# One strip task, longer assumed DMA latencies, planned clearing of V and an own buffer for fill blocks in a list-scheduled two-layer transformer kernel

## Chip, cores and metric

The kernel runs on one core of one Trainium2 chip. The metric is the device time of the whole program in microseconds (us). Several runs are quoted as a median with lowest and highest; ratios between kernels are explained in the result.

## The reference, cut to what matters

```python
def _A_ref(x, mem0, Wq, Wk, Wv, Wo, seg_len):     # attention with a recurrent memory
    mem = mem0                                    # 8 rows
    for s in range(n_seg):                        # 64 segments of 32 rows
        h = jnp.concatenate([mem, xs], axis=1)    # 40 rows, 512 columns
        q, k, v = ...                             # 32 heads of 128
        p = softmax(masked scores)
        o = (p @ v) @ Wo
        mem = o[:, :M, :]                         # the next segment needs it
        outs.append(o[:, M:, :])
def _B_ref(x, w_gate, w_up, w_down):
    return (sigmoid(x @ w_gate) * (x @ w_up)) @ w_down     # 512 -> 1792 -> 512
x = x + _A_ref(_layernorm(x), ...); x = x + _B_ref(_layernorm(x), ...)   # layer 1
x = x + _A_ref(_layernorm(x), ...); x = x + _B_ref(_layernorm(x), ...)   # layer 2, same weights
```

Inputs are bfloat16, x is 2048 by 512. The memory makes the 64 segments of a layer a chain. Layer 2 may run at the same time as layer 1, some segments behind it.

## The kernel before

A step handles one segment of layer 1 and, six steps behind, one of layer 2. There are 70 steps; in the first and last six only one layer has work, and matmuls have 40 instead of 80 columns. The kernel first records all work as tasks (engine, assumed duration, assumed latency until others see the result, what is read and written). A planner then simulates the engines and fixes the order of every engine. On the chip the order is fixed; real waits are semaphores. So an assumed latency costs nothing by itself: it decides only what stands before what.

```python
class Planner:
    LAT = {"PE": 205.0, "DVE": 110.0, "ACT": 128.0, "POOL": 40.0, "SP": 2200.0}
# ... setup
        self.xp = [self.xo[0], c.tile([P, D], BF16, name="xp1")]    # fill blocks; xo is the output tile too
        for t_ in self.qku:
            nc.gpsimd.memset(t_[:], 0.0)
        for t_ in self.vsb:
            nc.gpsimd.memset(t_[:], 0.0)
# ... in each step: V of the memory rows, with 32-column weights, four matmuls side by side
        def strips(q):
            for c in range(DC):
                for i in range(4):
                    k = 2 * i + q
                    nc.tensor.matmul(vb[q][32 * i:32 * i + 32, :], lhsT=hT[:, c, SCOL:SCOL + 32], rhs=self.wv[:, c, k * 512:(k + 1) * 512],
                                     start=(c == 0), stop=(c == DC - 1), skip_group_check=True)

        def add_strips():
            sb = pl.buf(self.sstp)
            for q in range(2):
                pl.add("PE", DC * (mm_ns(512) + 12) + 75, lambda q=q: strips(q), r=..., w=[vb[q]], use=[sb])
            for q in range(2):
                pl.add(("ACT", "DVE"), copy_ns(512), lambda q=q: (sb[:, q, :], vb[q][:, :]), ...)
            for i in range(4):                       # spread the strips into the V tiles
                pl.add("SP", 430, lambda i=i, vu=vu: nc.sync.dma_start(
                    out=self.vsb[vu][32:64, :], in_=sb[32 * i:32 * i + 32, :, :]), ..., lat=2600.0, use=[sb])
```

The other rows of V do not depend on the memory. They are computed ahead (V passes), stored to a scratch tensor in HBM (scr) and loaded into vsb before the step that needs them. For layer 2 that is a recurrence: feed-forward of a block in layer 1, V pass, store, load, product with the probabilities six steps later. A V pass of layer 2 fills 96 of 128 rows; the free 32 take a third of a "fill block" of layer 1 (blocks 6, 9, 12, 15), which so needs x loaded and normalized on its own.

Line numbers below: L674 strips, L704 q and k, L718 scores, L777 transposed probabilities, L788 their product with V, L805 output projection, L904 and L928 feed-forward, L568 V passes, L538 transposes. In the changed kernel all these are two or three lower: L672, L701, L715, L774, L785, L802, L901, L925, L566, L536. Tiles in the lines of the profile: sst holds the strips on their way to vsb, pb the probabilities, ptsb the transposed ones, otsb their product with V, xn a normalized input, hT a step's transposed input, xvf and xvl inputs of V passes, vst a finished part of V on its way to scr.

## Time and profile before

| | before |
|---|---|
| time, 3 runs | 1903.02 us (1902.42 to 1903.92) |
| profiled span | 1905.1 us, mean granted TensorE clock 0.992 |
| PE busy, idle | 1853.5 us, 51.6 us |
| VectorE, ScalarE, GpSimd busy | 67%, 63%, 30% |
| matmuls | 41250 |

"PE busy" is the union of the matmuls' slices, and ends are modelled: a lone matmul's slice is 0.2 us long, though its follower can start after 0.04 us. So a stall shorter than that leaves no idle time, and a longer one shows that much less. Starts are the better measure.

### The profile page before, as it was taken

To read this page: it belongs to the slowest core of one execution; us is meant where nothing else is said; L and a number is where in the kernel's file an instruction comes from. 1 tells how busy PE (TensorE), PEld (TensorE's weight loads), DVE (VectorE), ACT (ScalarE), POOL (GpSimd) and SP (SyncE) were. 2 spreads that over 40 slices of the span, in tenths; PEclk is the share of its full clock that TensorE was granted. 3 is DMA by queue.
4 is the path that set the end of the run, shared out by engine and by line. 5 is a ranking of instruction groups with operands and counts; after the bars stand their busy time and mean duration, and the time that the engine had idled before them with its cause. 6 is when DMAs were issued, how large, how long until landed. Compare 5 with 4: busy or idle time off the path is not lost.

```text
span 1905.1 us, 94394 instructions
## 1 busy us (share of the span) xinstructions
PE 1853.5 (97%) x41250; PEld 1579.6 (83%) x41250; DVE 1284.5 (67%) x4214; ACT 1192.4 (63%) x2722; POOL 580.1 (30%) x824
## 2 busy tenths in 40 slices
PE   7999899999999999989999999999999999999998
PEld 3578788988988888979888888988888898988786
DVE  5456577776777667756766777767776677766664
ACT  5655567666666666656665666666666666666554
POOL 5412012332424142332413232232413232333311
PEclk9999999999999999999999999999999999999999
DMA  9733324554635454544635454464635444454534
GB/s 350 243 92 106 86 61 141 149 155 118 185 106 165 116 168 127 155 138 128 179 84 172 120 155 140 128 178 134 174 97 167 128 137 141 134 161 138 161 94 139
DMA packets 133965, 273.84 MB, mean 144 GB/s; under 512 B 29254, under 2 KB 65358, under 8 KB 133550
## 3 DMA queue, kind: packets, MB, share of 16 engines
q0 software_dynamic: 59104, 181.61, 32.7%
q1 hardware_dynamic: 74446, 86.19, 15.7%
q8 instruction: 323, 5.29, 1.2%
q14 instruction: 92, 0.75, 0.1%
HBM read 222.04 MB, written 27.26 MB: 131 GB/s over the span
## 4 chain that ended last, share of the span: by engine, by line
PE 87%; DMA 4%; DVE 4%; issue 2%; ACT 2%; SPq 1%; POOL 1%; ACTq 0%; POOLq 0%; DVEq 0%
PE bank L704 30%; PE bank L805 15%; PE bank L904 10%; PE bank L568 8%; PE bank L674 6%; PE bank L928 5%; PE bank L718 5%; PE bank L788 4%; PE bank L777 3%; DMA vsb<-sst 2%; PE bank L538 1%; DMA scr<-vst 1%; DMA xo<-in_A_x_dram 1%; SPq L685 1%; DVE st L731 0%
## 5 line engine op out<-in xcount | busy, mean ns | idle before, releaser
L704 PE MATMUL bank<-hT,wq_sb 128*128 128x80 bf16 (+1 forms) x8960 | 624.8, 198 | 2.8 <-DVE hT L823 0.8
L704 PE MATMUL bank<-hT,wk_sb 128*128 128x80 bf16 (+1 forms) x8960 | 623.4, 198 | 0.4 <-issue 0.4
L996 ACT CAST qku<-bank 128x480 bf16<-128x480 f32 (+3 forms) x770 | 394.6, 512 | 259.3 <-PE bank L704 233.4
L704 PEld LDWEIGHTS <-wq_sb 128*128 128x128 bf16 x8960 | 458.5, 99 | 30.0 <-issue 10.0
L704 PEld LDWEIGHTS <-wk_sb 128*128 128x128 bf16 x8960 | 451.2, 99 | 1.3 <-issue 1.3
L731 DVE TENSOR_TENSOR st<-bank,maskb 80x240 f32<-80x240 f32 (+1 forms) x732 | 269.5, 369 | 196.0 <-PE bank L718 187.3
L805 PE MATMUL bank<-otsb,wo_sb 128*128 128x80 bf16 (+1 forms) x8960 | 375.7, 199 | 3.5 <-ACT otsb L996 2.7
L805 PEld LDWEIGHTS <-wo_sb 128*128 128x128 bf16 x8960 | 341.9, 100 | 14.2 <-issue 4.6
L896 POOL DMA_DIRECT2D wg<-in_B_w_gate_dram x217 | 164.4, 757 | 479.4 <-PE bank L904 430.1
L996 ACT CAST otsb<-bank 128x480 bf16<-128x480 f32 (+3 forms) x420 | 198.7, 486 | 106.2 <-PE bank L788 75.1
L922 POOL DMA_DIRECT2D wd<-in_B_w_down_dram x217 | 154.0, 711 | 221.1 <-PE bank L928 171.2
L526 POOL TENSOR_TENSOR lns<-lns,negh 128x1 f32<-128x1 f32 (+1 forms) x79 | 49.0, 621 | 531.0 <-DVE lns L525 430.1
L760 DVE TENSOR_TENSOR pb<-st,rz 80x480 bf16<-80x480 f32 x348 | 206.0, 593 | 4.4
L743 DVE TENSOR_REDUCE sm<-st 80x6 f32<-80x240 f32 (+3 forms) x420 | 152.8, 364 | 71.7 <-ACT st L741 69.6
L741 ACT ACTIVATE st<-st 80x240 f32<-80x240 f32 (+3 forms) x420 | 159.9, 381 | 27.5 <-DVE st L738 24.5
L718 PE MATMUL bank<-qku 128*80 128x80 bf16 (+1 forms) x2240 | 173.6, 203 | 1.3 <-ACT qku L996 0.3
L718 PEld LDWEIGHTS <-qku 128*80 128x80 bf16 (+1 forms) x2240 | 128.3, 117 | 55.4 <-ACT qku L996 17.0
L904 PE MATMUL bank<-xnT,wu 128*128 128x128 bf16 (+2 forms) x1784 | 171.3, 218 | 1.3 <-DMA wu<-in_B_w_up_dram 1.3
L904 PE MATMUL bank<-xnT,wg 128*128 128x128 bf16 (+2 forms) x1784 | 172.1, 219 | 0.0
L996 ACT CAST ptsb<-bank 128x480 bf16<-128x480 f32 (+3 forms) x277 | 134.5, 495 | 50.9 <-PE bank L777 46.8
L788 PE MATMUL bank<-ptsb,vsb 128*128 128x80 bf16 (+1 forms) x2240 | 141.7, 199 | 24.2 <-DMA vsb<-sst 10.4
L897 POOL DMA_DIRECT2D wu<-in_B_w_up_dram x217 | 163.0, 751 | 5.3 <-PE bank L904 1.6
(103 smaller groups left out, 2578.0 us busy)
## 6 DMA issues: line engine op xcount, KB each, us to landing
wg<-in_B_w_gate_dram POOLq DMA_DIRECT2D x219, 256.0 KB, 4.3
wd<-in_B_w_down_dram POOLq DMA_DIRECT2D x219, 256.0 KB, 4.8
wu<-in_B_w_up_dram POOLq DMA_DIRECT2D x218, 256.0 KB, 4.9
vsb<-scr SPq DMA_DIRECT2D x512, 48.0 KB
vsb<-sst SPq DMA_DIRECT2D x280, 64.0 KB
scr<-vst SPq DMA_DIRECT2D x128, 96.0 KB
wv_sb<-in_A_Wv_dram SPq DMA_DIRECT2D x4, 1024.0 KB
wq_sb<-in_A_Wq_dram SPq DMA_DIRECT2D x5, 768.0 KB
```

Source lines behind the costliest of these rows:

```text
L704: nc.tensor.matmul(o_ap, lhsT=W[:, c, h * P:(h + 1) * P], rhs=mv(c), start=(c == 0), stop=(c == DC - 1))
L718: nc.tensor.matmul(s_all(SB)[pr, uh - h0 + i, :], lhsT=qku[:, i, 0, 0:ncol], rhs=qku[:, i, 1, 0:ncol], start=True, stop=True)
L731: pl.add("DVE", dve_ns(n, True), lambda gsz=gsz, hs=hs, st=st, SB=SB, pj_=pj_, npj_=npj_, mk=mk, idx=idx: nc.vector.tensor_tensor(out=st[p ...
L741: pl.add("ACT", act_ns(n), lambda hs=hs, st=st: nc.scalar.activation(out=st[pr, hs], in_=st[pr, hs], func=ACTF.Exp, scale=self.scale), r=s ...
L760: nc.vector.tensor_tensor(out=o, in0=st[pr, hs].unsqueeze(1).to_broadcast([npart, 2, gsz, L]), in1=rz[pr, :, 0:gsz].unsqueeze(3).to_broadc ...
L788: nc.tensor.matmul(OB[:, hl * ncol:(hl + 1) * ncol], lhsT=self.vsb[(4 * t + h // 8) % 5][:, (h % 8) * P:(h % 8 + 1) * P], rhs=ptsb[:, hl, ...
L805: nc.tensor.matmul(WB[:, c * ncol:(c + 1) * ncol], lhsT=self.wo[:, h, c * P:(c + 1) * P], rhs=otsb[:, hl, 0:ncol], start=(h == 0 and c == ...
L896: pl.add("POOL", 760, lambda wg=wg, fs=fs: nc.gpsimd.dma_start(out=wg[:], in_=self.wgv[:, :, fs]), r=[("wo", self.H - 1)], w=[gk] + bt, la ...
L897: pl.add("POOL", 760, lambda wu=wu, fs=fs: nc.gpsimd.dma_start(out=wu[:], in_=self.wuv[:, :, fs]), r=[("wo", self.H - 1)], w=[uk] + bt, la ...
L904: nc.tensor.matmul(gu[:, 2 * i + k, 0:n], lhsT=W[:, c, i * P:(i + 1) * P], rhs=xnT[:, c, rw], start=(c == 0), stop=(c == DC - 1))
L922: pl.add("POOL", 760, lambda wd=wd, ip=ip: nc.gpsimd.dma_start(out=wd[:], in_=self.wdv[:, 2 * ip:2 * ip + 2, :]), w=[dk] + (["boot"] if se ...
L996: nc.scalar.copy(out=dst, in_=src)
```

## The change

The intent: keep the strips together, tell the planner how long DMAs really take, take clearing out of the fixed preamble, and free the fill blocks from the output tile. Cut to its core (the weights' latency is changed in four places, one shown):

```diff
-    LAT = {"PE": 205.0, "DVE": 110.0, "ACT": 128.0, "POOL": 40.0, "SP": 2200.0}
+    LAT = {"PE": 205.0, "DVE": 110.0, "ACT": 128.0, "POOL": 40.0, "SP": 4000.0}
 ...
-        self.xp = [self.xo[0], c.tile([P, D], BF16, name="xp1")]
+        self.xp = c.tile([P, D], BF16, name="xp")
 ...
         for t_ in self.hT:
-            nc.vector.memset(t_[:], 0.0)
-        for t_ in self.qku:
-            nc.gpsimd.memset(t_[:], 0.0)
+            nc.vector.memset(t_[:, :, L:2 * L], 0.0)
         for t_ in self.pb:
             nc.vector.memset(t_[:], 0.0)
-        for t_ in self.vsb:
-            nc.gpsimd.memset(t_[:], 0.0)
+        for k, t_ in enumerate(self.vsb):
+            self.pl.add("POOL", 950, lambda t_=t_: nc.gpsimd.memset(t_[:], 0.0), w=[("vs", k), ("vx", 0, k), ("vx", 1, k)])
 ...                                                                  # V stores
-                       lambda vs=vs, d=d, c0=c0, n=n: ("dma", d, vs[c0:c0 + BLK * n, 0:512 * w]), lat=2600.0 + 1500.0 * boot,
+                       lambda vs=vs, d=d, c0=c0, n=n: ("dma", d, vs[c0:c0 + BLK * n, 0:512 * w]), lat=4000.0 + 500.0 * boot,
 ...
-            i = self.nxt("xp", 2)
-            xb, key = self.xp[i], (("xo", 0) if i == 0 else "xp1")
+            xb, key = self.xp, "xp"
 ...
-        def strips(q):
-            for c in range(DC):
-                ...
+        def strips():
+            for q in range(2):
+                for c in range(DC):
+                    ...
-            for q in range(2):
-                pl.add("PE", DC * (mm_ns(512) + 12) + 75, lambda q=q: strips(q), r=hkeys + [("wv", h) for h in range(H)], w=[vb[q]], use=[sb])
+            pl.add("PE", 2 * DC * (mm_ns(512) + 12) + 150, strips, r=hkeys + [("wv", h) for h in range(H)], w=vb, use=[sb])
 ...                                                                  # strips into vsb
-                       r=[(sb, 0), (sb, 1)], w=[("vs", vu)], lat=2600.0, use=[sb])
+                       r=[(sb, 0), (sb, 1)], w=[("vs", vu)], lat=3500.0, use=[sb])
 ...                                                                  # weights, four places
-                pl.add("POOL", 760, lambda wg=wg, fs=fs: nc.gpsimd.dma_start(out=wg[:], in_=self.wgv[:, :, fs]), r=[("wo", self.H - 1)], w=[gk] + bt, lat=4000.0)
+                pl.add("POOL", 760, lambda wg=wg, fs=fs: nc.gpsimd.dma_start(out=wg[:], in_=self.wgv[:, :, fs]), r=[("wo", self.H - 1)], w=[gk] + bt, lat=6000.0)
```

## The prediction

> **What bounds the kernel now.** I read the page first, for the engines and the clock.
>
> ```profile
> PE 1853.5 (97%) x41250; PEld 1579.6 (83%) x41250; DVE 1284.5 (67%) x4214; ACT 1192.4 (63%) x2722; POOL 580.1 (30%) x824
> ...
> PE   7999899999999999989999999999999999999998
> ```
>
> TensorE (PE) is the bound: 97% busy in a 1905.1 us span, no other engine over 67%, idle 1905.1 - 1853.5 = 51.6 us. The table by stretch shows where: 23.8 us before 300 us, 19.4 us in the 1500 us after that, 9.3 us after 1800 us. So nothing that frees VectorE, ScalarE or GpSimd counts by itself. Only two things can: idle time of PE, and time that PE spends inside its "busy" on nothing. The waits of PE name the first kind, longest first:
>
> ```profile
> PE bank L788 <- DMA vsb<-sst: 10.4, 14, 2.1
> PE bank L509 <- DVE ident L445: 7.8, 1, 7.8
> PE bank L788 <- DVE ptsb L998: 7.7, 5, 5.7
> PE bank L538 <- ACT xn L529: 5.1, 3, 3.4
> ...
> PE bank L788 <- DMA scr<-vst: 1.8, 1, 1.8
> PE bank L904 <- DMA wu<-in_B_w_up_dram: 1.3, 1, 1.3
> ```
>
> Columns: total us, times, longest us. L788 is the product of probabilities and V. It waits 14 times for the strips of V that a DMA spreads from sst into vsb. For the second kind I read PE's instructions in order of time, start to start:
>
> ```profile
> 421.87 0.31 PE L704 MATMUL bank<-hT,wk_sb 128*128 128x80 bf16 x4
> 422.11 1.05 PE L674 MATMUL bank<-wv_sb,hT 128*32 128x512 bf16 x16
> 423.08 0.54 PE L718 MATMUL bank<-qku 128*80 128x80 bf16 x9
> ```
>
> Groups of four L704 follow each other every 0.14 to 0.15 us, but the strips (L674) start 0.24 us after the last: 0.10 us lost going in, none of it shown as idle. The 16 strip matmuls then take 0.97 us. The chain that ended last gives the same 0.98 us for 16 alone, and 1.84 us for 32 in one piece: 2 x 0.98 - 1.84 = 0.12 us is what leaving costs.
>
> **What the Trainium skill says.** "TensorEngine Tiling (Array Packing)", Key Properties: changing the tiling mode drains TensorE. Strips are the only matmuls with 32-column weights (128*32 above), so each group changes mode twice; the 0.10 and 0.12 us agree. "Perfetto Trace Analysis", Identifying the Most-Contended Engine: matmul busy share is no measure of what is left; true here, the drains lie inside the 97%. "DMA: Bandwidth & Descriptors", Anatomy of one DMA, fits about 2.0 us fixed plus bytes over 436 GB/s, for GpSimd-issued transfers. That is 2.15 us for 64 KB, but the strip transfers, issued from SyncE, end waits after 3.23, 4.90 and 5.04 us in the chain (at 429.61, 452.26, 584.26 us). The trace decides: the old plan's 2.6 us was short, 3.5 us is nearer and still short of some. "SBUF — State Buffer", Who interferes with whom: a VectorE cast in a 2-port mode and a GpSimd instruction exclude each other. The start of the trace shows it:
>
> ```profile
> 3.10 4.51 POOL L467 MEMSET vsb<- 128x1024 bf16 x5
> ...
> 3.66 4.04 DVE L445 CAST ident<-st 128x128 bf16<-128x128 f32 x1
> ```
>
> The cast of the identity lasts 4.04 us and ends 0.1 us after the last vsb clearing; PE's first matmul waits for it (7.8 us above).
>
> **The change part by part.** A list scheduler fixes every engine's order at build time from assumed durations, so most of the change is a new order. I compared the two built orders. PE has 41250 matmuls in both, the same by line.
>
> 1. *One strip task.* Before, the 70 steps' strips stand in 113 groups (27 of 32 matmuls, 86 of 16); after, in 70 groups of 32. 43 groups fewer x (0.10 to 0.13 in + 0.12 out, say 0.24) = **10.3 us**, all on PE, spread evenly. PE's runs of one line rise from 3032 to 3066, but other changes cost about 0.02 us each in the timeline: 0.7 us back or more.
>
> 2. *Longer latencies, strips to L788.* I added the PE work that stands between a step's last strip and its first L788, at the trace's rates (48 L704 in 1.72 us, 8 of 512 columns in 1.73 us, 16 L904 in 0.89 us). Before: median 4.4 us, 55 of 70 steps under 5.0 us, least 2.9. After: median 5.8 us, 2 of 70 under 5.0 us, least 4.1. Needed: a copy (0.59 us) plus 3.2 to 5 us landing plus queueing. So most of the 10.4 us goes: estimate **8 us**.
>
> 3. *Stores of V at 4.0 instead of 2.6 us, weights at 6.0 instead of 4.0 us.* These waits are worth 1.8 and 1.3 us. The last V store still has 7.5 us of PE work or so before its reader, as before. Gain **2.5 us**. The weights land in 4.3 to 4.9 us by the page, so 6.0 is cautious: it costs time in the plan, not on the chip unless the order gets worse.
>
> 4. *A buffer for fill blocks.* Fill blocks 6 and 12 used xo, which is also the output buffer.
>
> ```profile
> 806.02 4.09 DMA out_dram<-xo
> 810.11 0.02 issue
> 810.13 5.58 DMA xo<-in_A_x_dram
> ...
> 815.73 0.69 DVE lns L523
> 816.43 0.23 DVE ptsb L998
> ```
>
> The load waits for the store, VectorE stands behind the load, and the ptsb copy that PE needs stands behind VectorE: 5.7 us of PE idle, once. With its own buffer the load for that block is issued far ahead. The first fill block (90 us) costs PE 1.1 us in the same way; in the new order its statistics stand after the three ptsb copies. **6.8 us**.
>
> 5. *Clearing.* Three GpSimd qku memsets (0.49 us each alone, about 0.44 in a row) leave the queue, vsb's five stay ahead of everything: the identity cast can end 1.3 us earlier, and the start with it. **1.3 us**. The smaller hT memsets are VectorE time while it waits anyway: 0.
>
> Sum: 10.3 + 8 + 2.5 + 6.8 + 1.3 = 28.9 us. A new order of 41250 matmuls also brings waits that no view can show ahead; the old one had about 20 us in 1500 us of steady running, partly counted above. I put **5 us** against the sum: 1903 - 28.9 + 5 = **1879 us**, 1.3% faster.
>
> **The rivals.** *The recurrence becomes the bound.* Block b of layer 1 must pass the feed-forward, V, its store and its load before step 4b + 6 of layer 2. Cautious latencies could push that work late and PE would idle. For it: the feed-forward's tiles are triple-buffered and their planned pace falls. Against: the PE work between a block's last V pass and its reader is 5.0 to 7.5 us after, 6.8 to 8.4 before, nearly the same, and PE was over 98% busy from 300 to 1800 us. If it happened: waits of L788 on vsb<-scr, 10 to 30 us, no gain or a small loss. *The strip's wait was hidden anyway, or moves to ScalarE.* One task takes two banks at once and asks for two copies together, so L788 could wait on the copies. For: SyncE already waits 501.4 us for ACT's sst copies. Against: the distances in 2 are measured from the last strip. Then about 1888 us. *More comes back than counted*: fewer waits let feed-forward work fill the layer-1-only steps before 260 us, where much of the idle lies. Boot V work does move later in the new order (272 of 288 matmuls before the end of the first step, 260 after). Then 1865 us or less. *The clock*: it was 0.91 and 0.83 around 120 to 160 us; a denser PE could be throttled more, 2 to 5 us back.
>
> **Range and chances.** Items 1 and 4 (17 us) rest on counts and one clear chain, the other 12 us are likelier to be partly given back. With 4 to 20 us of new waits, or a few us more of gain, I get 1864 to 1894 us for 8 in 10. Faster by 2% needs under 1865 us, 38 us, nearly three quarters of all PE idle, so 0.12; slower by 2% would need the recurrence to break, 0.01.
>
> **What would show it.** Right: L674 in 70 pieces of 1.84 us and no isolated 0.98 us; the wait of L788 on vsb<-sst at 3 us or less; no VectorE wait for out_dram before a fill block; identity cast ending near 6.4 us; PE busy near 1843 us, idle near 37 us. Wrong: PE waiting on vsb<-scr or wg, wu, wd; a clock under 0.985; idle of PE not below 50 us; or a gain over 38 us, which would mean drains or hidden gaps bigger than 0.24 us a group.

## The result, and the profile after

| | before | after |
|---|---|---|
| time | 1903.01 us (1902.42 to 1903.92, 4 runs) | 1881.94 us (1877.41 to 1887.37, 4 runs) |
| profiled span | 1905.1 us | 1881.1 us |
| mean granted clock, profiled run | 0.992 | 0.996 |
| PE busy, idle | 1853.5, 51.6 us | 1838.7, 42.4 us |

The ratio is 0.989 (95% interval 0.9863 to 0.9917): the mean time of one kernel's fast runs over that of the other's of the same rounds, so not quite the ratio of the medians above. It is about 21 us, within the predicted range and within 2%.

The page of the changed kernel, engines, and PE by slice:

```profile
PE 1838.7 (98%) x41250; PEld 1582.1 (84%) x41250; DVE 1284.4 (68%) x4221; ACT 1176.9 (63%) x2715; POOL 576.9 (31%) x820
...
PE   7999999999999999999999999999999999999999
```

The 8s are gone and PE is still the bound. The waits of PE (columns: total us, times, longest us):

```profile
PE bank L785 <- DMA vsb<-scr: 6.8, 3, 2.8
PE bank L507 <- DVE ident L445: 6.4, 1, 6.4
PE bank L536 <- ACT xn L527: 5.8, 5, 3.4
PE bank L802 <- ACT otsb L993: 5.3, 11, 1.4
PE bank L774 <- DVE pb L757: 2.5, 10, 0.5
PE bank L701 <- DVE hT L815: 2.2, 6, 0.4
PE bank L785 <- DMA vsb<-sst: 1.8, 4, 0.7
```

Read against the list of before: the strips' wait (vsb<-sst) fell from 10.4 to 1.8 us, the wait for VectorE's ptsb copy from 7.7 to 0.2 us (below the lines shown), the identity from 7.8 to 6.4 us. New at the top is vsb<-scr, the recurrence, which had no wait in the list of before, and the output projection's wait for ScalarE doubled from 2.7 to 5.3 us. The strips, in order of time:

```profile
442.54 0.31 PE L701 MATMUL bank<-hT,wk_sb 128*128 128x80 bf16 x4
442.78 1.91 PE L672 MATMUL bank<-wv_sb,hT 128*32 128x512 bf16 x32
444.62 0.42 PE L715 MATMUL bank<-qku 128*80 128x80 bf16 x6
```

The way in costs 0.10 us as before (0.24 us after the start of the last four L701, where such groups follow each other in 0.14), then 32 matmuls take 1.84 us. The start, GpSimd and VectorE:

```profile
3.57 2.73 POOL L465 MEMSET vsb<- 128x1024 bf16 x3
...
3.00 3.38 DVE L445 CAST ident<-st 128x128 bf16<-128x128 f32 x1
```

The cast still ends with the clearing, now at 6.38 us. PE's first V pass starts at 12.62 us, before at 13.95 us.

### The clock

What the prediction did not put in its sum is the clock. These are stretches of the trace of before around the stall of 5.7 us at 810 us (columns: stretch, length, busy time with counts of PE, PEld, DVE, ACT, POOL, then granted clock, DMA share, GB/s):

```profile
814.00:816.00 2.00, 0.00 (x0) 0.00 (x0) 0.27 (x1) 0.00 (x0) 0.00 (x0) 1.00 0.96 302
816.00:818.00 2.00, 1.29 (x21) 1.29 (x21) 1.22 (x5) 0.29 (x1) 0.00 (x0) 0.58 0.24 77
818.00:820.00 2.00, 2.00 (x24) 1.47 (x23) 0.23 (x1) 0.43 (x2) 0.00 (x0) 0.57 0.06 18
820.00:822.00 2.00, 2.00 (x58) 2.00 (x56) 0.45 (x2) 0.74 (x2) 1.28 (x2) 1.00 0.26 51
```

After the stall the granted clock is little more than half over some 4 us. The stall costs its idle time and then 2 x 0.42 + 2 x 0.43 = 1.7 us of clock, as much as 3.4 us at half clock. In steps of 10 us the trace of before has nine places under full clock (130 to 160, 190, 810, 970, 1810, 1870 and 1880 us), that of after four of any size (140, 320, 1170 and 1800 us). The Trainium skill has this in "TensorE: Matmul & The Clock Gate", Part 1: TensorE's clock halves when it was idle for a window of about 3.4 us and returns after about as long a busy one, and the windows run freely. The trace agrees on the half clock and its length. It does not agree on the cause: of the eight stretches of half clock in the trace of before that begin within the span, only the one at 816 us follows 3.4 us without a matmul. In the 3.4 us before each of the others the profile has PE busy for 1.76 us or more, before the one at 147 us all the time, by ends that are modelled. Two of these stretches of 3.41 us, before 147 us and before 816 us:

```profile
143.88:147.29 3.41, 3.41 (x94) 2.98 (x89) 2.59 (x9) 2.57 (x10) 0.00 (x0) 1.00 0.36 82
812.89:816.30 3.41, 0.00 (x0) 0.00 (x0) 0.57 (x1) 0.00 (x0) 0.00 (x0) 1.00 0.93 294
```

What sets off the others is not shown; see the last section.

Over all runs the mean clock was 0.9925 for the kernel before (33 runs) and 0.9970 for the changed one (4 runs). Span x (1 - clock) is a rough measure of the time lost: 15.2 us in the profiled run of before, 7.5 us in that of after. Runs of one and the same kernel show the link: 1.4 us more per 0.001 less clock (slope within kernels, 102 runs, correlation 0.67). One plan, null_after below, took 1874.03 us at a mean clock of 1.000 and 1893.93 us at 0.994. The clock alone makes about 11 us of these 20 (0.006 of the span).

### A ledger

To see where time went I split each profiled span in four. *Work* is every matmul of the built order at rates of the trace (27840 with 80 columns at 35.8 ns, 5760 with 40 at 26.4, 3912 with 128 at 55.7, 1262 with 512 at 216.5, 2240 strips at 54, 236 of other sizes, and 0.24 us per group of strips). *Idle* is the sum of PE's waits that name a releaser. *Clock* is span x (1 - clock). The rest holds what is too short to show.

| profiled run | span | work | idle | clock | rest |
|---|---|---|---|---|---|
| before | 1905.1 | 1796.0 | 43.2 | 15.2 | 50.7 |
| after | 1881.1 | 1785.7 | 35.2 | 7.5 | 52.7 |
| difference | -24.0 | -10.3 | -8.0 | -7.7 | +2.0 |

The split is mine, an account and not a measurement: "work" falls by 10.3 us because 43 groups fewer are counted at 0.24 us, and a stall lowers the clock as well, so "clock" is partly the price of idle time. "Idle" falls by only 8.0 us although some 23 us of the waits of before went (vsb<-sst 8.6, ptsb 7.5, mx 2.3, scr<-vst 1.8, the identity 1.4, wu 1.3). So about 15 us of new ones came.

### The profile page after: what moved, and what is told of

It is laid out like the page before. It is cut to its first block, busy times and chain, and to the rows that moved or that the text cites. A ratio compares the mean times of both kernels' runs of the same rounds, so it can differ in the third digit from the quotient of the medians.

```text
span 1881.1 us, 94528 instructions
## 1 busy us (share of the span) xinstructions
PE 1838.7 (98%) x41250; PEld 1582.1 (84%) x41250; DVE 1284.4 (68%) x4221; ACT 1176.9 (63%) x2715; POOL 576.9 (31%) x820
## 4 chain that ended last, share of the span: by engine, by line
PE 87%; DVE 3%; ACT 2%; DMA 2%; issue 1%; SPq 0%; POOL 0%; ACTq 0%; DVEq 0%; POOLq 0%
PE bank L701 32%; PE bank L802 14%; PE bank L901 10%; PE bank L672 7%; PE bank L566 6%; PE bank L925 5%; PE bank L715 5%; PE bank L774 4%; PE bank L785 4%; DMA vsb<-sst 1%; ACT otsb L993 1%; PE bank L536 1%; DMA scr<-vst 1%; DMA vsb<-scr 1%; DVE st L728 1%
## 5 line engine op out<-in xcount | busy, mean ns | idle before, releaser
L701 PE MATMUL bank<-hT,wq_sb 128*128 128x80 bf16 (+1 forms) x8960 | 624.5, 198 | 3.3 <-DVE hT L815 2.2
L701 PE MATMUL bank<-hT,wk_sb 128*128 128x80 bf16 (+1 forms) x8960 | 623.1, 198 | 0.2 <-issue 0.2
L701 PEld LDWEIGHTS <-wq_sb 128*128 128x128 bf16 x8960 | 458.3, 99 | 26.8 <-issue 6.8
L701 PEld LDWEIGHTS <-wk_sb 128*128 128x128 bf16 x8960 | 450.8, 99 | 0.3 <-issue 0.3
L802 PE MATMUL bank<-otsb,wo_sb 128*128 128x80 bf16 (+1 forms) x8960 | 371.4, 198 | 6.9 <-ACT otsb L993 5.3
L740 DVE TENSOR_REDUCE sm<-st 80x6 f32<-80x240 f32 (+3 forms) x420 | 152.2, 363 | 51.6 <-ACT st L738 49.7
L993 ACT CAST ptsb<-bank 128x480 bf16<-128x480 f32 (+3 forms) x295 | 144.2, 497 | 47.2 <-PE bank L774 44.7
L908 DVE SCALAR_TENSOR_TENSOR hff<-th,bank 128x256 bf16<-128x256 f32 (+2 forms) x231 | 94.1, 407 | 104.4 <-ACT th L906 101.9
```

What stands on the lines that cost most here:

```text
L701: nc.tensor.matmul(o_ap, lhsT=W[:, c, h * P:(h + 1) * P], rhs=mv(c), start=(c == 0), stop=(c == DC - 1))
L740: pl.add("DVE", dve_ns(n), lambda hs=hs, st=st, sm=sm: nc.vector.tensor_reduce(out=sm[pr, hs], in_=st[pr, hs], axis=AX.X, op=ALU.add), r=s ...
L802: nc.tensor.matmul(WB[:, c * ncol:(c + 1) * ncol], lhsT=self.wo[:, h, c * P:(c + 1) * P], rhs=otsb[:, hl, 0:ncol], start=(h == 0 and c == ...
L993: nc.scalar.copy(out=dst, in_=src)
```

## The experiments

Theory: the gain is the sum of countable parts (drains, waits). Rivals: it is one lucky plan; it is one part; the parts are hidden and the order alone matters. All runs gave correct results. "us" is (ratio - 1) x 1908 us, the mean of before. Groups are strip groups in the built order, "under 5" the steps with less than 5.0 us of PE work between strips and their reader. An interval reaches 3 to 5 us to each side. The experiments ran on three chips, so rows are compared through their ratios to before; the difference of two rows is uncertain by up to 6 us or so.

| run | ratio to before (95%) | us | groups | under 5 | clock, mean |
|---|---|---|---|---|---|
| null_latency | 1.0028 (1.0006 to 1.0050) | +5.3 | 108 | 56 | 0.991 |
| only_strip | 0.9957 (0.9933 to 0.9981) | -8.2 | 70 | 34 | 0.995 |
| only_lat | 0.9991 (0.9967 to 1.0014) | -1.7 | 131 | 7 | 0.996 |
| only_xp | 0.9996 (0.9968 to 1.0023) | -0.8 | 107 | 54 | 0.992 |
| the change | 0.9890 (0.9863 to 0.9917) | -21.0 | 70 | 2 | 0.997 |
| no_strip | 0.9978 (0.9964 to 0.9992) | -4.2 | 132 | 8 | 0.996 |
| no_lat | 0.9972 (0.9957 to 0.9988) | -5.3 | 70 | 38 | 0.995 |
| no_xp | 0.9906 (0.9890 to 0.9921) | -17.9 | 70 | 2 | 0.996 |
| ident_act | 0.9885 (0.9868 to 0.9903) | -21.9 | 70 | 2 | 0.995 |
| fixed_fill | 0.9971 (0.9956 to 0.9986) | -5.5 | 113 | 55 | 0.994 |
| split_drain | 0.9993 (0.9977 to 1.0009) | -1.3 | 140 | 2 | 0.996 |
| null_after | 0.9874 (0.9846 to 0.9901) | -24.0 | 70 | 2 | 0.996 |
| later_load | 0.9889 (0.9873 to 0.9905) | -21.2 | 70 | 3 | 0.994 |

### How much a new plan alone does: null_latency, null_after

A null is a run that changes nothing that should matter; what it shows is the scatter that plans have by themselves.

```diff
-    LAT = {..., "SP": 2200.0}      # before
+    LAT = {..., "SP": 2260.0}
```

> The kernel before with one assumed latency nudged (SyncE 2200 to 2260 ns): no part of the change, but a new plan. It has 108 strip groups instead of 113 (5 x 0.24 = 1.2 us less) and the same distances from strips to L788. Theory (gains come from countable parts): about 1902 us, within 4 us of before. Rival (any new order scatters by 10 us or more, and the 21 us are luck): off by 8 us or more in either direction.

Measured: 5.3 us slower (1914.83 us, clock 0.991). The theory's 4 us were too tight. The interval is wide, 1 to 10 us, and it is one null. A plan that differs in nothing intended moved the time by 5 us here, so no difference of that size between replanned kernels says much.

```diff
-    LAT = {..., "SP": 4000.0}      # after
+    LAT = {..., "SP": 4060.0}
```

> The changed kernel with one assumed latency nudged (SyncE 4000 to 4060 ns): another plan, a quarter of the rows stand elsewhere, all counts equal (70 strip groups, 2 steps under 5.0 us). Theory: within 5 us of the changed kernel, ratio to before 0.9865 to 0.9915. Rival (the 21 us are one lucky plan): 0.993 or more.

Measured: 0.9874, 24 us faster than before, 1886.11 us (1874.03 to 1893.93) on that chip. The gain is no accident of one plan. The waits on vsb<-scr do depend on the plan: 12.2 us in the profiled run of null_after (its slowest), 6.8 in the changed kernel.

### The drains by themselves: split_drain

```diff
             for q in range(2):
+                if q:
+                    nc.tensor.matmul(vb[1][:, 0:16], lhsT=self.ident[:, :], rhs=self.ident[:, 0:16], start=True, stop=True)
                 for c in range(DC):
```

> The changed kernel with a full-width matmul of 16 columns between the two halves of every strip task; its result is overwritten by the second half, the order is otherwise the same. Theory (each mode change pair costs 0.24 us): 70 x (0.24 + 0.03) = 19 us more than the changed kernel, about 1901 us, ratio to before near 0.999; strips take 0.98 us twice. Rival (the drains fill waits that are there anyway): 8 us more or less, ratio under 0.994.

Measured: 0.9993. Against the changed kernel's 0.989 that is 19.7 us more, 14 to 26 by the two intervals; 19 were expected. The trace of split_drain in order of time:

```profile
444.41 1.05 PE L674 MATMUL bank<-wv_sb,hT 128*32 128x512 bf16 x16
445.39 0.18 PE L670 MATMUL bank<-ident 128*128 128x16 bf16 x1
445.50 1.05 PE L674 MATMUL bank<-wv_sb,hT 128*32 128x512 bf16 x16
446.48 0.42 PE L717 MATMUL bank<-qku 128*80 128x80 bf16 x6
```

The strips take from 444.41 to 446.48, 2.07 us instead of 1.84: 0.23 us for the two mode changes and the small matmul. The order was not replanned, so this is the cleanest number: a pair of mode changes costs at most 0.23 us where it stands (the small matmul is in it), and 70 of them make 16 of the 19.7 us. What the engine does in that time, a drain or the loading of other weights, the run does not tell apart.

### Strips alone, and the change without them: only_strip, no_strip

```diff
-            for q in range(2):
-                pl.add("PE", DC * (mm_ns(512) + 12) + 75, lambda q=q: strips(q), ..., w=[vb[q]], use=[sb])
+            pl.add("PE", 2 * DC * (mm_ns(512) + 12) + 150, strips, ..., w=vb, use=[sb])
```

(no_strip is the reverse in the changed kernel.)

> The kernel before plus the single strip task alone. 113 groups become 70: 43 x 0.24 = 10.3 us. Steps with under 5.0 us of PE work between strips and L788 fall from 55 to 34, so a few us of vsb<-sst waits go as well. Theory: 1903 - 10.3 - 3 = about 1890 us. Rival (drains are hidden or the two copies that now come together make L788 wait): 1898 us or more, with waits of L788 on sst copies or vsb<-sst at 10 us or more.

> The changed kernel with the strips in two tasks again. 132 strip groups instead of 70: 62 x 0.24 = 14.9 us more. Distances as in the changed kernel (8 of 70 steps under 5.0 us instead of 2). Theory: 1882 + 15 = about 1897 us. Rival (merging matters only through order): under 1890 us.

Measured: alone -8.2 us (13 expected, at the edge of the interval, 4 to 13); taken away from the change, 16.8 us come back (15 expected). In only_strip the waits for sst still add to 8.2 us, and the fill block's stall is there as a wait of 4.7 us for hT. An effect not foreseen: with both banks filled at once, the two copies of the strips go to two engines. The instructions on sst in the kernel before, then in the changed one:

```profile
L996 ACT CAST sst<-bank x131: 561/585/605, 29.7 to 1872.5; 128x512 bf16<-128x512 f32 x131
L998 DVE CAST sst<-bank x9: 675/692/693, 142.0 to 1850.2; 128x512 bf16<-128x512 f32 x9
```

```profile
L993 ACT CAST sst<-bank x76: 562/586/592, 29.0 to 1845.6; 128x512 bf16<-128x512 f32 x76
L995 DVE CAST sst<-bank x64: 673/679/693, 28.2 to 1844.7; 128x512 bf16<-128x512 f32 x64
```

131 to 9 became 76 to 64 (82 to 58 in only_strip): ScalarE, which also makes the copies that the output projection waits for, has 55 fewer.

### Latencies alone, and the change without them: only_lat, no_lat

```diff
-    LAT = {..., "SP": 2200.0}
+    LAT = {..., "SP": 4000.0}
-    lat=2600.0 + 1500.0 * boot     # V stores
+    lat=4000.0 + 500.0 * boot
-    lat=2600.0                     # strips into vsb
+    lat=3500.0
-    lat=4000.0                     # feed-forward weights
+    lat=6000.0
```

> The kernel before plus the longer latencies alone. The plan splits strips more (131 groups instead of 113: 18 x 0.24 = 4.3 us more) but only 7 of 70 steps have under 5.0 us between strips and L788 (55 before): 8 us of vsb<-sst waits and 2.5 us of others go. Theory: 1903 + 4.3 - 10.5 = about 1897 us. Rival (latencies are the main cause of the gain): 1890 us or less.

> The changed kernel with the old assumed latencies. Still 70 strip groups; 38 of 70 steps under 5.0 us (2 in the changed kernel), so 4 to 6 us of vsb<-sst waits come back; the new waits on vsb<-scr (6.8 us in the changed kernel) go, as the least PE work between V pass and reader rises from 5.1 to 6.3 us. Theory: 1880 to 1885 us, the latencies net near nothing beside one strip task. Rival (latencies carry half of the gain): 1890 us or more.

Measured: alone -1.7 us; taken away from the change, 15.7 us come back. Both expectations missed, the second by more than 10 us: its rival was right. The lines of PE's waits in only_lat show what stood against the gain:

```profile
PE bank L805 <- ACT otsb L996: 13.0, 22, 2.5
...
PE bank L788 <- DMA vsb<-scr: 5.7, 6, 2.0
PE bank L788 <- DMA vsb<-sst: 2.0, 5, 0.8
```

The strips' wait is at 2.0 us as meant. But the plan now splits the strips in 131 groups (4.3 us), and PE waits 13.0 us for ScalarE's otsb copies, 2.7 before; no_strip has 12.3 us of the same wait. Only together with one strip task is it 5.3 us. In no_lat the opposite half is missing: vsb<-sst is back at 10.3 us. So the two parts are not additive. Why otsb is late is not shown: ScalarE's copies of strips are not enough as a reason, since only_lat leaves it 122 of them, nine fewer than before, and has the longer wait. No run moved those copies alone. The latencies also bring waits of the recurrence: vsb<-scr is 5.7 us in only_lat and none before; but no_lat, without them, still has 3.2 us, which its expectation had put at none.

The ledger for these (columns as above):

| profiled run | span | work | idle | clock | rest |
|---|---|---|---|---|---|
| only_strip | 1902.1 | 1785.7 | 44.1 | 9.5 | 62.8 |
| only_lat | 1910.9 | 1800.3 | 45.5 | 11.5 | 53.6 |
| no_strip | 1900.5 | 1800.6 | 39.6 | 9.5 | 50.8 |
| no_lat | 1898.7 | 1785.7 | 41.2 | 9.5 | 62.3 |

The rest is 10 us larger in the two kernels with one strip task and short latencies. I have no cause for it, so more than half of the 15.7 us that no_lat loses stays unexplained. (The profiles of the experiments miss up to 233 of 41250 matmul records, so their PE busy time is not compared; the ledger does not use it.)

### The fill buffer: only_xp, no_xp, fixed_fill

```diff
-        self.xp = [self.xo[0], c.tile([P, D], BF16, name="xp1")]
+        self.xp = c.tile([P, D], BF16, name="xp")
-            i = self.nxt("xp", 2)
-            xb, key = self.xp[i], (("xo", 0) if i == 0 else "xp1")
+            xb, key = self.xp, "xp"
```

(only_xp in the kernel before; no_xp is the reverse in the changed one.) fixed_fill leaves the plan of before untouched and only moves block 12's load to a tile that is free:

```diff
+            if b == 12:
+                xb = fview(self.xvf[0][:, 0, 0:1], [(1, self.D)])
             self.load_x(b, xb, key, ...)
```

> The kernel before plus the buffer for fill blocks alone. 107 strip groups instead of 113 (1.4 us less), the VectorE wait for the store and the load gone (5.7 us of PE idle; 1.1 us more if the first fill block moves too). Theory: 1895 to 1896 us. Rival (the recurrence or another wait takes it up): 1900 us or more.

> The changed kernel with xo shared by fill blocks again; strip groups and distances the same (70, 2 under 5.0 us). Theory: the wait of VectorE for the output store comes back, PE idles 4 to 6 us: about 1887 us. Rival (cautious latencies alone move the load early enough): within 2 us of the changed kernel.

> The kernel before in exactly its old order on every engine; only fill block 12 is loaded into a tile that is long free (xvf) instead of xo. Theory: the PE stall of 5.7 us at 810 us goes, and with it the stretch of half clock that follows it (clock 0.50 to 0.65 from 816 to 820 us, 1.7 us of clock time): 7 to 8 us in all, a ratio near 0.996 to 0.9965. Rival 1 (a stall costs only its idle time): 5.7 us, 0.997. Rival 2 (the recurrence takes the time back at once, as the kernel with the buffer alone and a new plan seemed to say): under 3 us.

Measured: only_xp -0.8 us with runs from 1903.7 to 1917.0, inconclusive beside a null of 5 us. Its trace has the load of block 12 issued at 414 us, long before it is read at 730 us, and no wait of VectorE at 810 us, so the stall went, but the time did not follow. no_xp gives back 3.1 us, less than the intervals can tell from nothing, and VectorE's waits show the old line again:

```profile
DVE lns L521 <- DMA xo<-in_A_x_dram: 4.1, 1, 4.1
```

fixed_fill is the clean one: -5.5 us (3 to 8 by its interval), less than the theory's 7 to 8 and no more than rival 1's 5.7. The time alone therefore does not decide between them; the trace says more. The stall did not vanish but fell from 5.68 to 2.08 us, because the load, no longer blocked, still stands late in SyncE's order (issued at 810 us, right after the store). The clock after it differs too. The same stretches in fixed_fill:

```profile
814.00:816.00 2.00, 0.41 (x2) 0.10 (x1) 0.48 (x1) 0.07 (x1) 1.90 (x3) 1.00 1.01 278
816.00:818.00 2.00, 1.51 (x35) 1.39 (x36) 1.10 (x6) 0.29 (x1) 0.00 (x0) 1.00 1.02 313
818.00:820.00 2.00, 1.95 (x49) 1.88 (x49) 0.20 (x2) 0.79 (x3) 1.28 (x2) 1.00 0.90 270
```

Full clock after it. 3.6 us of idle and 1.7 us of clock make 5.3 us; measured 5.5. That fit is loose: the same profiled run has half clock from 437 us on, after a stall of 1.72 us that the trace of before does not have. Where half clock falls changes from one execution to the next, so one trace cannot put a price on one stall.

### The start: ident_act

```diff
-        nc.vector.tensor_copy(out=self.ident[:], in_=identf)
+        nc.scalar.copy(out=self.ident[:], in_=identf)
```

> The changed kernel with the identity cast on ScalarE; the order of PE is the same. Theory (VectorE's cast lasts 3.4 us only because GpSimd clears V at the same time): ScalarE casts in under 0.4 us, PE's first matmul starts at 4 us or earlier instead of 6.4, the V passes start 2 us or more earlier and the run ends 2 to 3 us earlier, 1879 to 1880 us. Rival (the start is bound by the loads of x or the first weights): the first V pass moves by under 0.7 us, no gain.

ScalarE cast in 0.30 us (3.38 us on VectorE in the changed kernel), and the first V pass came 2.16 us earlier:

```profile
10.46 3.60 PE L566 MATMUL bank<-wv_sb,xvf 128*128 128x512 bf16 x8 [0.36 <-ACT xvf L993]
```

That fits, but does not prove, the exclusion of VectorE and GpSimd, which "SBUF — State Buffer", Who interferes with whom, describes: ScalarE, which shares no port with GpSimd there, cast from 2.36 to 2.66 us, while GpSimd's preamble ran on until 6.30 us. But the long clearing began only at 2.62 us, so the two hardly overlapped. The stronger sign is in the changed kernel: VectorE's cast starts at 3.00 us, three clearings start after it (from 3.57 us), and it ends 0.08 us after the last of them. In the whole time (-21.9 against -21.0 us) 2 us cannot be told from the spread; the trace shows the start, not the end. GpSimd's clearing remains in the way: its first layer-norm instruction starts at 6.28 us, as soon as the clearing ends.

### A better plan?: later_load

```diff
-        w=[("vx", j, vu)], lat=6000.0)      # loads of V; with ident_act's edit
+        w=[("vx", j, vu)], lat=9500.0)
```

> The changed kernel with the identity cast on ScalarE and 9500 instead of 6000 ns assumed for the loads of V: the least PE work between a V pass and its reader rises from 5.1 to 8.0 us, its median from 7.7 to 10.9, strip groups stay 70. Theory: the 6.8 us of waits on vsb<-scr and the three half-clock stretches after them (3 x 1.7 us) go, and 2 us at the start: about 1870 us, ratio near 0.982. Rival (the V work pulled ahead delays the feed-forward, and PE waits elsewhere): 1878 us or more, with waits on hT, otsb or the weights above 10 us.

Measured: -21.2 us, no better; the rival had the time right (1887 us, it said 1878 or more), though none of the waits that it named passed 10 us. PE's waits in later_load:

```profile
PE bank L536 <- ACT xn L527: 8.6, 6, 5.0
PE bank L802 <- ACT otsb L993: 8.1, 23, 0.7
PE bank L566 <- ACT xvl L993: 4.4, 10, 0.5
```

vsb<-scr is gone altogether (6.8 us in the changed kernel), but otsb went from 5.3 to 8.1 and xvl from 0.8 to 4.4 us, and the mean clock was 0.994. The likely reason is that the V work pulled ahead took ScalarE's time from the step's chain; no run tests that by itself. No tried version beats the change clearly; null_after's 0.9874 lies within its interval.

Clearing alone was not run; its effect is read in the traces of the start (1.3 us).

## Why the prediction was right

The time, 1882 us, was predicted as 1879 us. The forecast of the time was right, partly by luck. By its own steps:

1. *One strip task, 10.3 us.* Right: 70 pieces, 1.84 us in the trace, and split_drain measured the pair, with its small matmul, at 0.23 us in place. That copies move to VectorE was not foreseen.
2. *Strips to their reader, 8 us.* Right in the trace: 10.4 to 1.8 us, 8.6 us. That this gain needs the one strip task (only_lat: -1.7 us) was not foreseen; the steps were summed as if independent.
3. *Stores and weights, 2.5 us.* Wrong. The two old waits (1.8 and 1.3 us) went, but three waits on vsb<-scr came, 6.8 us: the recurrence, which the rivals named and the text held unlikely because the distances were nearly equal. "PE waiting on vsb<-scr" was the prediction's own sign of being wrong, and it came. The slip is in the distance: step 3 says "7.5 us or so, as before", the rivals' paragraph 5.0 to 7.5 us after and 6.8 to 8.4 before, and neither is held against what the way through HBM takes. At 323 us that is a store of 3.69 us followed by a load of 3.02 us, 6.7 us in all, more than 5.0. Taken by waits the step is a net loss of 3.7 us instead of a gain, though not all of the 6.8 us is due to the latencies (3.2 stay in no_lat).
4. *Fill buffer, 6.8 us.* Right in the trace, 7.5 us of the wait for ptsb gone. As a share of the total less certain: 3.1 us by no_xp, 5.5 us by fixed_fill.
5. *Clearing, 1.3 us.* Right: 13.95 to 12.62 us.
6. *New waits, 5 us.* Too small: about 15 us, with vsb<-scr, already counted in step 3, nearly half of it.
7. *The clock.* The sum had no term for it, and the rival had the sign wrong: a denser PE would be throttled more. It rose from 0.992 to 0.996 in the profiled runs, worth up to 7.7 us. Steps 2 to 6 had idle time falling by 13.6 us; by the ledger it fell by 8.0, and the rest rose by 2.0, which makes 7.6 us missing. The clock made up for just that, which is luck: the total was closer than its steps deserve. Idle of PE was put at 37 us and was 42.4.

Two small readings of the prediction are off. PE's idle time after 1800 us is 8.4 us, not 9.3 (the three parts must add to 51.6). And the strips are not quite the only matmuls with 32-column weights: 18 more stand in the last feed-forward block.

## What to carry to other kernels

Where a planner fixes the order, change one assumption that should not matter and measure first: here that null was 5 us, more than several parts of the change. Test a mechanism in a kernel whose order stays the same (fixed_fill, split_drain); those two can be read in the trace where they stand, while the parts with new plans did not add up. And count a TensorE stall with what follows it: the one of 5.7 us was paid again in 1.7 us of half clock.

## What the Trainium skill lacked or had wrong

- "TensorE: Matmul & The Clock Gate", Why this matters for your kernels, advises no idle gaps over about 3 us. At 971 us of the kernel before, a stall with 1.82 us of idle was followed by a clock of 0.50 (974 to 976 us); in fixed_fill one of 2.08 us, at 814 us, was not. Here the limit is not safe, and the length of a stall alone does not decide. (Another section of that page, on a second failure mode, does let frequent short idle bring back the half clock, without a length.)
- The same page, Part 1, has the half clock begin after an idle window. Seven of eight stretches in the trace of before began without one (see The clock).
- The same page, Part 1, puts the penalty of warming up at under 1% of a typical span. All half clock in the run of before, most of it long after the start, comes to 0.8% (15.2 of 1905.1 us). What is missing: plans of one program differ in it (mean clock 0.9907 to 0.9970) by as much as a tuning step gains.
- "TensorEngine Tiling (Array Packing)", Key Properties, says that a mode change drains TensorE but gives no cost: here 0.10 us going in, 0.12 us coming out, and 0.23 us for a pair with a small matmul between in split_drain.
- "DMA: Bandwidth & Descriptors", Anatomy of one DMA, has a fit for transfers that GpSimd issues; an estimate from it is 2.15 us for 64 KB. In the chain of before, strip transfers from SyncE, 64 KB each, ended waits after 2.00 to 6.13 us, with other transfers under way.
